# The last block of a channel-attention and SwiGLU kernel: twelve plain matmuls a step in place of twenty-one short ones

## The chip, the cores and the metric

The program runs on one core of one Trainium2 chip. The time is device microseconds (us) from the program's start to its end, lower is better. The core's engines have queues of their own, each worked off in order: TensorE (PE; its weight loads are shown apart as PEld), VectorE (DVE), ScalarE (ACT), GpSimd (POOL) and SyncE (SP), which only issues DMAs.

## The reference

```python
qn = q / (norm(q, axis=1) + 1e-6);  kn = k / (norm(k, axis=1) + 1e-6)     # (2, 6016, 256)
a = softmax(kn^T @ qn / tau)                                             # (2, 256, 256)
x = (v @ a).reshape(12032, 256)
xn = x / sqrt(mean(x*x) + 1e-6) * rms_g
out = (silu(xn @ w_gate) * (xn @ w_val)) @ w_out                         # d_ff = 1536
```

Everything is float32.

## The kernel before

A float32 operand is kept as the sum of two tiles of a rounded format (fp32r), a high and a low one, and a product of two operands is three matmuls: high by high, high by low, low by high. To make a pair of tiles out of a float32 tile, ScalarE copies it to the high tile and VectorE or GpSimd writes the difference to the low one.

The 12032 rows are 94 tiles of 128, worked off in 24 blocks: block 0 and block 23 have three tiles (384 columns of the transposed rows), the others four. In a block, step f = 0 to 11 makes a slice of 128 of the 1536 hidden columns, and five steps later (`LAG = 5`) that slice's part of the output is multiplied by `w_out` into PSUM.

There are two ways to compute a step. Blocks 0 and 1 are plain (`emit_hidden`): for gate and value, two slices of the 256 input columns times three matmuls, that is 12 matmuls over all columns of the block. Blocks 2 to 23 use a Strassen-Winograd scheme (`emit_step`): 7 products, each of three matmuls over half the columns (256, in block 23 it is 192), 21 in all. Its weight sums lie in the tiles `s` (`s_hl`), and for each pair p of steps the fourth sum has overwritten a quarter of the weights of step 2p+1 in place (`build_s`, the tile `w`). The output matmuls of some pairs use such a scheme too, and the plain output weights that it overwrote are restored in the last block by `restore_so`.

`emit_step` is a pipeline of three steps: at step f it runs products 7, 2 and 4 of step f-2, products 3 and 6 of step f-1 and products 5 and 1 of step f. Product 4 writes over a PSUM half (tile `pu`) that VectorE must have read before (line 771, the tiles `zg` and `zv`):

```python
product(7, u[:, 1])
...
nc.vector.tensor_tensor(out=z[:, 1:], in0=u, in1=t[:, :2], op=ALU.add)   # line 771
...
product(4, u[:, 1])
```

Line 772 adds product 2 (tile `pq`), line 790 multiplies gate by value for three of the four quarters, line 799 for the last. Line 696 turns the result for the output scheme (`run_turned`). `round_pair` then has it split into the pairs `gx`, `gy`, `gz`: ScalarE copies (line 704), GpSimd subtracts (line 710; on VectorE only for the last pair of block 23). `run_later` issues the parts of a pair that were put off. `post_copy`, `post_sums`, `post_out` and `post_store` read a finished block's output from PSUM (lines 931, 941, 950), turn it and store it; the next block writes to the same PSUM banks.

The order on every engine is the order in which the code issues (a manual schedule); the tables `steady`, `steady_mid` and `extra` say which side work follows which step. An instruction that waits holds up all that stand behind it on its engine.

Of the kernel before, what the change touches and what calls it, by code (L numbers as in the profile page):

```python
# [8 lines left out]
F32 = mybir.dt.float32  # L9
F32R = mybir.dt.float32r  # L10
# [5 lines left out]
P = 128  # L16
# [3 lines left out]
def kernel(  # L20
# [68 lines left out]
    def f32(ap):  # L89
        return ap.bitcast(F32)  # L90
# [469 lines left out]
    def emit_xT_round(j, i):  # L560
        h = blocks[j][2] * P // 2
# [103 lines left out]
    def round_pair(j, p, zg, h):  # L665

        x, y = new_g("x", 3, j, 2 * p), new_g("y", 2, j, 2 * p + 1)
        engine = nc.vector if (j, p) == (NB - 1, NP - 1) else nc.gpsimd
        w = [[w[:, 2 * p + i, e * P:(e + 1) * P] for w in wo] for i in range(2) for e in range(2)]
        if strassen(j, p):  # L670
            z = new_g("z", 2, j, 2 * p + 1)
# [12 lines left out]
        else:  # L684
            rounds.append((zg[:, 1:3], *(by_quarter(t, 2, h) for t in x), engine))
            later.append((zg[:, 0:4:3], *(by_quarter(t, 2, h) for t in y), engine))
            for i, g in enumerate((x, y)):
                if j == NB - 1:
                    G[j, 2 * p + i] = g
                    continue  # L690
# [118 lines left out]
    def new_state(j, f):  # L809
# [2 lines left out]
        t = pool["z"].tile([P, 3 * HN], F32, tag="t", name=f"t_{j}_{f}")  # L812
        return j, f, h, product, u, t[:, :3 * h].rearrange("p (i n) -> p i n", i=3)

    def emit_hidden(j, f, between=()):
        nt = blocks[j][2]
        n = nt * P
# [2 lines left out]
        for wj, nm in enumerate("gv"):  # L820
# [7 lines left out]
                    )  # L828
                    m += 1
            ps.append(t)  # L830
        if "z" not in pool:
# [7 lines left out]
        nc.vector.tensor_tensor(out=hh[:, :n], in0=th[:, :n], in1=ps[1][:, :n], op=ALU.mult)  # L839
        for go in between[1:]:  # L840
            go()
        tag = "xyz"[(j * NF + f) % 3]
        gh, gl = new_g(tag, 3 if tag == "x" else 2, j, f)
        rounds.append((hh[:, :n], gh[:, :n], gl[:, :n], nc.gpsimd if j else nc.vector))
        run_rounds()
        run_subs()
        G[j, f] = (gh, gl)
# [126 lines left out]
    with tc.manual_schedule():  # L974
# [128 lines left out]
        def at(j, f, go):  # L1103
            extra.setdefault((j, f), []).append(go)
# [51 lines left out]

        for i, f in enumerate((7, 7, 8)):
            at(NB - 1, f, lambda i=i: restore_so(i))

        def new_so():  # L1160
            so_hl.extend(
# [145 lines left out]
            go(0)  # L1307
            go(1)

        for i, (j, f) in enumerate(steps + [(None, None)] * 2):  # L1310
            outs = []
            if j is not None:
                owed.append((i + (2 if j < WINO else LAG), j, f))
            while owed and (owed[0][0] <= i or j is None and len(outs) < 2 and owed[0][1:] in G):
                outs.append(owed.pop(0)[1:])
            k = min(j, 5) if j is not None else None
            hooks = [
                [lambda go=go: go(j) for go in table[k].get(f, ())] if j is not None else []
                for table in (pres, mids, ends)
            ]  # L1320
# [52 lines left out]
```

## Time and profile before

| | |
|---|---|
| runs | 1266.56 us median of 3 (1266.0 to 1269.39) |
| the profiled execution | 1264.47 us, span 1262.7 us from its first to its last instruction |
| TensorE's granted clock | 0.999 of full speed |
| busy share of the span | PE 99%, PEld 94%, DVE 70%, ACT 69%, POOL 64% |
| block 23 | from about 1207 us to the end of the span |

A busy share is a mean over the span. Where one engine is busy nearly throughout, the others matter where it waits for them; a row of the timeline gives an instruction's start, its duration and, in square brackets, how long its engine stood idle before it and what ended that.

### The profile page before, as it was taken

How to read it: one execution, taken by the hardware profiler on the slowest of the kernel's cores; microseconds unless marked ns; L12 is line 12 of the kernel's file. 1: busy time of each engine (PE TensorE's matmuls, PEld its weight loads, DVE VectorE, ACT ScalarE, POOL GpSimd, SP SyncE). 2: the span in 40 equal slices, each digit the busy share in tenths (PEclk: the TensorE clock that was granted, in tenths of full speed). 3: DMA queues.
4: the chain of work that ended last, by engine and by line, in shares of the span. 5: the costliest groups of instructions: out<-in, count | busy, mean ns of one | idle time of the engine just before them, and what ended most of it. 6: DMA issues, size and time to landing. Idle time of an engine off the chain costs nothing.

```text
span 1262.7 us, 25136 instructions
## 1 busy us (share of the span) xinstructions
PE 1250.5 (99%) x9225; PEld 1191.4 (94%) x9225; DVE 885.8 (70%) x1573; ACT 868.4 (69%) x1771; POOL 803.5 (64%) x639
## 2 busy tenths in 40 slices
PE   8999999999999999999999999999999999999998
PEld 7799988999999999999999999999999999999998
DVE  5889698658767657667766766766676676676664
ACT  5667557667777787777767777777767767777654
POOL 0120355675777777777777777777877777777652
PEclk9999999999999999999999999999999999999999
DMA  8969111020220220211211211202202202101101
GB/s 305 321 215 288 31 35 49 19 36 18 52 34 18 50 35 18 47 33 24 44 25 35 39 29 36 38 21 45 35 18 51 35 18 51 30 18 30 18 1 30
DMA packets 223964, 71.77 MB, mean 57 GB/s; under 512 B 186592, under 2 KB 215392, under 8 KB 223840
## 3 DMA queue, kind: packets, MB, share of 16 engines
q1 hardware_dynamic: 223008, 68.92, 23.4%
q8 instruction: 72, 1.18, 0.4%
q10 hardware_dynamic: 832, 1.25, 0.3%
q14 instruction: 52, 0.43, 0.1%
HBM read 46.40 MB, written 12.32 MB: 47 GB/s over the span
## 4 chain that ended last, share of the span: by engine, by line
PE 91%; DVE 3%; DMA 2%; ACT 1%; SPq 1%; issue 1%; POOL 0%; POOLq 0%; ACTq 0%; DVEq 0%
PE pu L742 44%; PE po L916 26%; PE pq L742 7%; PE px L443 5%; PE s L180 3%; DMA raw<-in_k_dram 2%; PE po L866 2%; PE pg L825 1%; PE pv L825 1%; DVE wk L599 1%; SPq L532 1%; ACT sq L195 1%; DVE acc L204 0%; DVE zh L839 0%; PE pn L222 0%
## 5 line engine op out<-in xcount | busy, mean ns | idle before, releaser
L742 PE MATMUL pu<-xt,w 128*128 128x256 f32 (+1 forms) x2376 | 407.0, 280 | 0.4 <-DVE zv L771 0.3
L742 PE MATMUL pu<-xt,s 128*128 128x256 f32 (+1 forms) x2376 | 366.2, 280 | 0.9 <-ACT t L778 0.8
L742 PEld LDWEIGHTS pu<-xt,w 128*128 128x128 f32 x2376 | 343.8, 188 | 14.1 <-DVE zg L771 1.1
L742 PEld LDWEIGHTS pu<-xt,s 128*128 128x128 f32 x2376 | 326.8, 189 | 13.5 <-ACT t L778 1.0
L710 POOL TENSOR_TENSOR gy<-zg,gy 128x512 fp32r<-128x512 f32 (+1 forms) x131 | 181.6, 1386 | 150.3 <-ACT gy L704 82.9
L710 POOL TENSOR_TENSOR gx<-zg,gx 128x512 fp32r<-128x512 f32 (+2 forms) x131 | 200.3, 1529 | 83.0 <-ACT gx L704 82.8
L783 ACT ACTIVATE t<-pu 128x512 f32<-128x512 f32 (+1 forms) x264 | 156.9, 594 | 99.6 <-PE pu L742 83.1
L916 PE MATMUL po<-gx,w 128*128 128x256 f32 (+1 forms) x927 | 197.1, 330 | 0.0
L771 DVE TENSOR_TENSOR zv<-pu,t 128x512 f32<-128x512 f32 (+1 forms) x132 | 89.7, 679 | 102.7 <-ACT zg L805 76.8
L778 ACT ACTIVATE t<-pu 128x256 f32<-128x256 f32 (+1 forms) x264 | 100.1, 379 | 88.8 <-PE pu L742 87.1
L790 DVE TENSOR_TENSOR zg<-zg,zv 128x768 f32<-128x768 f32 (+1 forms) x132 | 150.0, 1136 | 13.7
L704 ACT ACTIVATE gx<-zg 128x512 fp32r<-128x512 f32 (+2 forms) x132 | 95.2, 721 | 71.7 <-DVE zg L799 37.0
L696 DVE TENSOR_TENSOR zg<-zg 128x256 f32<-128x256 f32 x228 | 97.0, 426 | 67.4 <-POOL gx L710 61.5
L916 PEld LDWEIGHTS po<-gx,w 128*128 128x128 f32 x927 | 136.4, 188 | 6.3 <-ACT os L952 0.2
L742 PE MATMUL pq<-xt,w 128*128 128x256 f32 (+1 forms) x792 | 135.7, 280 | 0.0
L771 DVE TENSOR_TENSOR zg<-pu,t 128x512 f32<-128x512 f32 (+1 forms) x132 | 89.0, 674 | 44.6 <-PE pu L742 29.1
L799 DVE TENSOR_TENSOR zg<-pu,zg 128x256 f32<-128x256 f32 (+1 forms) x132 | 55.6, 421 | 90.4 <-PE pu L742 88.6
L916 PE MATMUL po<-gy,w 128*128 128x512 f32 x414 | 118.1, 393 | 0.0
L710 POOL TENSOR_TENSOR gz<-zg,gz 128x512 fp32r<-128x512 f32 x57 | 114.1, 2001 | 0.0
L742 PEld LDWEIGHTS pq<-xt,w 128*128 128x128 f32 x792 | 111.9, 189 | 0.0
L787 ACT ACTIVATE zg<-zg 128x768 f32<-128x768 f32 (+1 forms) x132 | 109.5, 829 | 0.0
L572 POOL TENSOR_TENSOR xt<-xp,xt 128x512 fp32r<-128x512 f32 (+1 forms) x44 | 69.4, 1601 | 31.7 <-ACT xt L570 31.7
(146 smaller groups left out, 2051.7 us busy)
## 6 DMA issues: line engine op xcount, KB each, us to landing
v<-in_v_dram SPq DMA_DIRECT2D x84, 128.0 KB, 3.6
xnT<-xw SPq DMA_DIRECT2D x336, 32.0 KB, 1.9
out_dram<-ob SPq DMA_DIRECT2D x84, 128.0 KB, 3.2
raw<-in_q_dram SPq DMA_DIRECT2D x20, 512.0 KB, 4.9
raw<-in_k_dram SPq DMA_DIRECT2D x19, 512.0 KB, 5.9
wraw<-in_moe_w_gate_dram SPq DMA_DIRECT2D x12, 256.0 KB, 4.9
wraw<-in_moe_w_val_dram SPq DMA_DIRECT2D x12, 256.0 KB, 5.8
wraw<-in_moe_w_out_dram SPq DMA_DIRECT2D x12, 256.0 KB, 5.9
```

The costliest lines, as they stand in the source:

```text
L443: nc.tensor.matmul(out=px[:, i, :], lhsT=w[:, c, i * P:(i + 1) * P], rhs=x[:, c, :], start=(i == 0 and c == 0 and m == 0), stop=(c == KC - ...
L572: nc.gpsimd.tensor_tensor(out=o, in0=x, in1=f32(y), op=ALU.subtract)
L696: nc.vector.tensor_tensor(out=z[:, o], in0=z[:, i0], in1=z[:, i1], op=ALU.subtract)
L704: nc.scalar.activation(out=gh, in_=hh, func=AF.Copy)
L710: engine.tensor_tensor(out=gl, in0=hh, in1=f32(gh), op=ALU.subtract)
L742: nc.tensor.matmul(out=out, lhsT=wm[wi], rhs=xm[xi], start=(start and q == 0), stop=(q == 2), skip_group_check=True,)
L771: nc.vector.tensor_tensor(out=z[:, 1:], in0=u, in1=t[:, :2], op=ALU.add)
L778: nc.scalar.activation(out=mt[:, 0], in_=mu[:, 1], func=AF.Copy)
L783: nc.scalar.activation(out=nt[:, 1:], in_=nu, func=AF.Copy)
L787: nc.scalar.activation(out=zg[:, 1:], in_=zg[:, 1:], func=AF.Silu)
L790: nc.vector.tensor_tensor(out=zg[:, 1:], in0=zg[:, 1:], in1=z, op=ALU.mult)
L916: nc.tensor.matmul(out=acc[b][:, o:o + g.shape[-1]], lhsT=w, rhs=g, start=first, stop=True, skip_group_check=True,)
```

## The change

Block 23 is computed plainly. Its three tiles of input are split once as a whole (`emit_xT_round` calls `split`; the seven sums of the scheme fall away, `emit_xT_parts` returns). In its steps 0 and 1 the pipeline of block 22 is first run empty (`emit_step(None, None, ...)`), then `emit_hidden` issues the 12 matmuls of 384 columns. Steps 2 to 11 are `emit_hidden` and one output each. The two empty rounds of the pipeline behind the last step fall away. In block 23 VectorE, not GpSimd, subtracts for the low tile, and the split results lie in tiles that are no longer needed (`last_g`).

What the scheme had overwritten must be put back first: `restore_s(p)` computes the weights of step 2p+1 from three sums on VectorE, has ScalarE copy the high tile and VectorE write the low one. It stands behind steps 7 and 9 of block 22 (p = 0, 1) and behind steps 0, 2, 6 and 9 of block 23 (p = 2 to 5); step 2p+1 of block 23 needs it.

```diff
     def emit_xT_round(j, i):
+        if j == NB - 1:
+            if i == 0:
+                new_xT(j)
+                split(moved[j][:, :, :blocks[j][2] * P], xT[j], nc.gpsimd)
+            return
...
-        engine = nc.vector if (j, p) == (NB - 1, NP - 1) else nc.gpsimd
+        engine = nc.gpsimd
...
+    def restore_s(p):
+
+        t = pool["wk"].tile([P, 2, 2 * P], F32, tag="wk", name=f"wr_{p}")
+        wh, wl = (w[:, :, :2 * P] for w in w_hl)
+        sh, sl = (x[:, p, 0] for x in s_hl)
+        nc.vector.tensor_tensor(out=t[:, 0], in0=f32(wh[:, 2 * p]), in1=f32(wl[:, 2 * p]), op=ALU.add)
+        nc.vector.tensor_tensor(out=t[:, 1], in0=f32(sh), in1=f32(sl), op=ALU.add)
+        nc.vector.tensor_tensor(out=t[:, 0], in0=t[:, 0], in1=t[:, 1], op=ALU.subtract)
+        nc.scalar.activation(out=wh[:, 2 * p + 1], in_=t[:, 0], func=AF.Copy)
+        nc.vector.tensor_tensor(
+            out=wl[:, 2 * p + 1], in0=t[:, 0], in1=f32(wh[:, 2 * p + 1]), op=ALU.subtract
+        )
...
-        tag = "xyz"[(j * NF + f) % 3]
-        gh, gl = new_g(tag, 3 if tag == "x" else 2, j, f)
-        rounds.append((hh[:, :n], gh[:, :n], gl[:, :n], nc.gpsimd if j else nc.vector))
+        if j == NB - 1:
+            gh, gl = last_g(f)
+        else:
+            tag = "xyz"[(j * NF + f) % 3]
+            gh, gl = new_g(tag, 3 if tag == "x" else 2, j, f)
+        engine = nc.gpsimd if 0 < j < NB - 1 else nc.vector
+        rounds.append((hh[:, :n], gh[:, :n], gl[:, :n], engine))
...
+        for p, f in enumerate((7 - NF, 9 - NF, 0, 2, 6, 9)):
+            at(NB - 1 + f // NF, f % NF, lambda p=p: restore_s(p))
...
-        for i, (j, f) in enumerate(steps + [(None, None)] * 2):
+        for i, (j, f) in enumerate(steps):
...
-            if j is not None and j < WINO:
+            if j < WINO or j == NB - 1:
+                if j == NB - 1 and f < 2:
+                    emit_step(None, None, i % 2, outs)
+                    outs = []
+                elif j == NB - 1 and f == 2:
+                    run_later()
                 emit_hidden(j, f, weights.get((j, f), ()))
+                for go in hooks[1]:
+                    go()
                 for o in outs:
                     emit_all(o)
```

The change moves instructions on VectorE at two kinds of places. The first is VectorE's queue at step 7 of block 22, where step 5's results are finished and step 6's begin (line 799 is the last of step 5, line 771 the first of step 6). Before:

```order
L790 TENSOR_TENSOR zg_4_15307<-zg_4_15307,zv_5_15357 128x768 [waits DVE_49,Activation_49]
L799 TENSOR_TENSOR zg_4_15307<-pu_5_15251,zg_4_15307 128x256 [waits PE_49,Activation_49]
L771 TENSOR_TENSOR zg_6_15402<-pu_6_15298,t_6_15299 128x512 [waits PE_49,Activation_49,Pool_49]
L772 TENSOR_TENSOR zg_6_15402<-pq_6_15398,t_6_15299 128x256 [waits PE_49]
L696 TENSOR_TENSOR zg_4_15307<-zg_4_15307 128x256 [waits Pool_49]
L696 TENSOR_TENSOR zg_4_15307<-zg_4_15307 128x256 [waits DVE_49] x3
L771 TENSOR_TENSOR zv_7_15447<-pu_7_15346,t_7_15347 128x512 [waits PE_49,Activation_49]
```
After the change lines 771, 772, 790 and 799 have the numbers 775, 776, 794 and 803, and the four instructions of `restore_s(0)` are lines 842 to 846:

```order
L794 TENSOR_TENSOR zg_4_15301<-zg_4_15301,zv_5_15347 128x768 [waits DVE_49,Activation_49]
L803 TENSOR_TENSOR zg_4_15301<-pu_5_15245,zg_4_15301 128x256 [waits PE_49,Activation_49]
L842 TENSOR_TENSOR wr_15383<-w_97,w_98 128x256
L843 TENSOR_TENSOR wr_15383<-s_1413,s_1414 128x256
L844 TENSOR_TENSOR wr_15383<-wr_15383 128x256 [waits DVE_49]
L846 TENSOR_TENSOR w_98<-wr_15383,w_97 128x256 [waits Activation_49]
L775 TENSOR_TENSOR zg_6_15398<-pu_6_15292,t_6_15293 128x512 [waits PE_49,Pool_49]
L776 TENSOR_TENSOR zg_6_15398<-pq_6_15394,t_6_15293 128x256 [waits PE_49]
L700 TENSOR_TENSOR zg_4_15301<-zg_4_15301 128x256 [waits Pool_49]
```
Four instructions now stand between step 5's last and step 6's first, and the fourth of them waits for ScalarE. The same holds behind step 9 with `restore_s(1)`.

The second place is VectorE's queue where block 23 begins. `pu_11` is the PSUM tile of block 22's step 11, `pu_0` that of block 23's step 0. Before:

```order
L696 TENSOR_TENSOR zg_8_15496<-zg_8_15496 128x256 [waits DVE_49] x3
L771 TENSOR_TENSOR zv_11_15647<-pu_11_15535,t_11_15536 128x512 [waits PE_49,Activation_49]
L772 TENSOR_TENSOR zv_11_15647<-pq_11_15643,t_11_15536 128x256 [waits PE_49]
L790 TENSOR_TENSOR zg_10_15596<-zg_10_15596,zv_11_15647 128x768 [waits DVE_49,Activation_49]
L799 TENSOR_TENSOR zg_10_15596<-pu_11_15535,zg_10_15596 128x256 [waits PE_49,Activation_49]
L771 TENSOR_TENSOR zg_0_15693<-pu_0_15587,t_0_15588 128x384 [waits PE_49,Activation_49,Pool_49]
```
After, `zh_0` is step 0's plain result (line 876), `glast_0` its low tile (line 714), and `wr` belongs to `restore_s(2)`:

```order
L700 TENSOR_TENSOR zg_8_15498<-zg_8_15498 128x256 [waits DVE_49] x3
L876 TENSOR_TENSOR zh_0_15641<-zh_0_15641,pv_0_15634 128x384 [waits PE_49,Activation_49]
L714 TENSOR_TENSOR glast_0_15645<-zh_0_15641,glast_0_15644 128x384 [waits Activation_49]
L842 TENSOR_TENSOR wr_15648<-w_97,w_98 128x256
L843 TENSOR_TENSOR wr_15648<-s_1413,s_1414 128x256
L844 TENSOR_TENSOR wr_15648<-wr_15648 128x256 [waits DVE_49]
L846 TENSOR_TENSOR w_98<-wr_15648,w_97 128x256 [waits Activation_49]
L775 TENSOR_TENSOR zv_11_15665<-pu_11_15537,t_11_15538 128x512 [waits PE_49]
L776 TENSOR_TENSOR zv_11_15665<-pq_11_15661,t_11_15538 128x256 [waits PE_49]
L794 TENSOR_TENSOR zg_10_15596<-zg_10_15596,zv_11_15665 128x768 [waits DVE_49]
```
The reading of `pu_11`, which stood directly behind `run_turned` (line 696, now 700), now stands behind block 23's step 0, its split and a restoration.

## Rows read from the trace of the kernel before

**Rows 1.** The page's busy times (part 1): busy us, share of the span, instructions.
```profile
PE 1250.5 (99%) x9225; PEld 1191.4 (94%) x9225; DVE 885.8 (70%) x1573; ACT 868.4 (69%) x1771; POOL 803.5 (64%) x639
```

**Rows 2.** Waits from 1207 us on, TensorE's weight loads: total us, times, longest.
```profile
PEld po L866 <- POOL gy L710: 0.6, 1, 0.6
PEld pu L742 <- DVE zg L771: 0.3, 1, 0.3
PEld po L866 <- DVE gx L710: 0.3, 1, 0.3
PEld po L866 <- ACT gx L704: 0.3, 1, 0.3
```

**Rows 3.** Timeline, TensorE's weight loads in block 23: start, us, engine, line, tiles.
```profile
1228.85 0.75 PEld L742 LDWEIGHTS pu<-xt,s 128*128 128x128 f32 x6
...
1229.86 0.78 PEld L866 LDWEIGHTS po<-w,gy 128*128 128x128 f32 x6
...
1230.57 0.42 PEld L742 LDWEIGHTS pu<-xt,w 128*128 128x128 f32 x3
...
1232.27 0.75 PEld L742 LDWEIGHTS pu<-xt,s 128*128 128x128 f32 x6
```

**Rows 4.** Timeline, TensorE in block 0, matmuls of 384 columns.
```profile
119.13 1.20 PE L825 MATMUL pv<-xt,w 128*128 128x384 f32 x6
120.17 1.23 PE L866 MATMUL po<-w,gx 128*128 128x256 f32 x9
```

**Rows 5.** Timeline of all engines, block 22, step 7.
```profile
1190.72 0.42 DVE L799 TENSOR_TENSOR zg<-pu,zg 128x256 f32<-128x256 f32 x1
...
1191.27 0.85 ACT L704 ACTIVATE gx<-zg 128x768 fp32r<-128x768 f32 x1 [1.01 <-DVE zg L799]
...
1192.19 1.85 POOL L710 TENSOR_TENSOR gx<-zg,gx 128x768 fp32r<-128x768 f32 x1 [0.35 <-ACT gx L704]
...
1193.73 0.54 PEld L742 LDWEIGHTS pu<-xt,w 128*128 128x128 f32 x3
```

**Rows 6.** Timeline of all engines, block 22, step 9.
```profile
1197.06 2.01 POOL L710 TENSOR_TENSOR gz<-zg,gz 128x512 fp32r<-128x512 f32 x1
...
1198.33 0.42 DVE L799 TENSOR_TENSOR zg<-pu,zg 128x256 f32<-128x256 f32 x1 [0.41 <-PE pu L742]
...
1199.80 1.84 POOL L710 TENSOR_TENSOR gx<-zg,gx 128x768 fp32r<-128x768 f32 x1 [0.73 <-ACT gx L704]
...
1201.26 0.42 PEld L742 LDWEIGHTS pu<-xt,w 128*128 128x128 f32 x3
```

**Rows 7.** Lines 605 and 602: count, duration in ns as min/median/max, starts.
```profile
L605 DVE TENSOR_TENSOR w<-wk,w x6: 421/1513/1517, 163.6 to 226.9; 128x256 fp32r<-128x256 f32 x6
L602 ACT ACTIVATE w<-wk x6: 403/419/422, 161.6 to 224.9; 128x256 fp32r<-128x256 f32 x6
```

**Rows 8.** Timeline, the restoring of out weights that the kernel already has.
```profile
1235.53 1.32 POOL L710 TENSOR_TENSOR gx<-zg,gx 128x384 fp32r<-128x384 f32 x1 [2.40 <-ACT gx L704]
...
1236.02 1.25 DVE L646 TENSOR_TENSOR wback<-wback,wback 128x384 f32<-128x384 f32 x1
...
1237.78 0.41 PEld L742 LDWEIGHTS pu<-xt,w 128*128 128x128 f32 x3 [0.31 <-DVE zg L771]
```

**Rows 9.** Groups by form, block 0's chain at 384 columns: busy us, mean ns.
```profile
L836 ACT ACTIVATE th<-pg 128x384 f32<-128x384 f32 x12 | 5.8, 479 | 0.0
...
L839 DVE TENSOR_TENSOR hh<-th,pv 128x384 f32<-128x384 f32 x12 | 6.5, 545 | 0.0
...
L704 ACT ACTIVATE gx<-hh 128x384 fp32r<-128x384 f32 x4 | 2.1, 525 | 3.4 <-DVE hh L839 3.4
...
L710 DVE TENSOR_TENSOR gx<-hh,gx 128x384 fp32r<-128x384 f32 x4 | 2.2, 547 | 0.0
```

**Rows 10.** Timeline, block 22's sums on VectorE.
```profile
1224.52 1.29 DVE L950 TENSOR_TENSOR os<-po,os 128x512 f32<-128x512 f32 x2 [0.70 <-PE po L916]
```

**Rows 11.** Windows, the end: us; busy us of PE, PEld, DVE, ACT, POOL; PEclk; DMA.
```profile
1258.00:1262.70 4.70, 0.33 (x3) 0.13 (x2) 0.42 (x1) 0.27 (x1) 0.00 (x0) 0.77 0.32 84
```

More of the change, by code (lines that the diff above doesn't have):

```diff
@@ L560, in emit_xT_round @@
     def emit_xT_round(j, i):
+        if j == NB - 1:
+            if i == 0:
+                new_xT(j)
+                split(moved[j][:, :, :blocks[j][2] * P], xT[j], nc.gpsimd)
+            return
         h = blocks[j][2] * P // 2
@@ L687, in round_pair @@
             for i, g in enumerate((x, y)):
-                if j == NB - 1:
-                    G[j, 2 * p + i] = g
-                    continue
                 G[j, 2 * p + i] = [(e, 0, w[2 * i + e], [t[:, :2 * h] for t in g]) for e in range(2)]
@@ L813, in new_state, with last_g @@
         return j, f, h, product, u, t[:, :3 * h].rearrange("p (i n) -> p i n", i=3)
+    spare = {}
+    def last_g(f):
+        n = BN
+        if 4 <= f < 8:
+            if f == 4:
+                spare["xt"] = [
+                    xt_p.tile([P, XS * HN], F32R, tag=f"xt{i}", name=f"glast{i}") for i in range(2)
+                ]
+            n = XS * HN // 4
+            return [x[:, (f - 4) * n:(f - 3) * n] for x in spare["xt"]]
+        if f % 4 < 2:
+            p, tag = ((vt_p, "vt"), (sm_p, "a"))[f % 4]
+            return [p.tile([P, n], F32R, tag=f"{tag}{i}", name=f"glast{i}_{f}") for i in range(2)]
+        x = xn_p.tile([P, 2, n], F32R, tag=("xn", "moved")[f % 2], name=f"glast_{f}")
+        return [x[:, i] for i in range(2)]
+    def restore_s(p):
[9 more added lines that the diff above has]
+        )
     def emit_hidden(j, f, between=()):
@@ L830, in emit_hidden @@
             ps.append(t)
-        if "z" not in pool:
+        if (j, f) == (NB - 1, 0):
+            th = hh = v_p.tile([P, BN], F32, tag="vw", name=f"zh_{j}_{f}")
+        elif "z" not in pool:
             th, hh = (pool["h"].tile([P, BN], F32, tag=y, name=f"{y}_{j}_{f}") for y in ("th", "hh"))
@@ L841, in emit_hidden @@
             go()
-        tag = "xyz"[(j * NF + f) % 3]
-        gh, gl = new_g(tag, 3 if tag == "x" else 2, j, f)
-        rounds.append((hh[:, :n], gh[:, :n], gl[:, :n], nc.gpsimd if j else nc.vector))
+        if j == NB - 1:
+            gh, gl = last_g(f)
[4 more added lines that the diff above has]
+        rounds.append((hh[:, :n], gh[:, :n], gl[:, :n], engine))
         run_rounds()
@@ L1308, in emit_all @@
             go(1)
-        for i, (j, f) in enumerate(steps + [(None, None)] * 2):
+        for i, (j, f) in enumerate(steps):
             outs = []
-            if j is not None:
-                owed.append((i + (2 if j < WINO else LAG), j, f))
-            while owed and (owed[0][0] <= i or j is None and len(outs) < 2 and owed[0][1:] in G):
+            owed.append((i + (2 if j < WINO else LAG), j, f))
+            while owed and owed[0][0] <= i:
                 outs.append(owed.pop(0)[1:])
-            k = min(j, 5) if j is not None else None
+            k = min(j, 5)
             hooks = [
-                [lambda go=go: go(j) for go in table[k].get(f, ())] if j is not None else []
-                for table in (pres, mids, ends)
-            ]
-            if j is not None and j < WINO:
+                [lambda go=go: go(j) for go in table[k].get(f, ())] for table in (pres, mids, ends)
+            ]
+            if j < WINO or j == NB - 1:
[4 more added lines that the diff above has]
+                    run_later()
                 emit_hidden(j, f, weights.get((j, f), ()))
+                for go in hooks[1]:
+                    go()
                 for o in outs:
@@ L1332 @@
                 go()
-            for go in extra.get((j, f), []) if j is not None else []:
+            for go in extra.get((j, f), []):
                 go()
-        run_later()
         owed = [emit_out(*o[1:]) for o in owed]
```

## Prediction

> **What bounds the kernel now.** I read the page's busy times first: TensorE is busy 99% of the span [rows 1], so what counts is the length of its queue and every wait in it; the other engines cost something only where it waits for them. Next came the waits of the stretch that changes, from 1207 us to the end: its weight loads waited 0.6 us for GpSimd and three times 0.3 us, 1.5 us in all [rows 2]. Then the timeline, for the price of a step. In block 23 the same group of six weight loads starts at 1228.85 and again at 1232.27, so a step takes 3.42 us [rows 3]. Its six output matmuls take the time to the next group, 1230.57 - 1229.86 = 0.71, so 0.118 each; nine take 1.06. The 21 products of 192 columns have the other 2.36 us, 0.112 each.
>
> The plain form is in the trace too, in block 0 with the same 384 columns: six start at 119.13, the next group at 120.17, so 0.173 each and 2.08 for twelve [rows 4].
>
> **What is gained.** 2.36 - 2.08 = 0.28 a step, 3.3 us over 12 steps. The last pairs, which had to come through the pipeline's two empty rounds, were what TensorE waited for in rows 2; a plain step's result is ready while four other outputs are still to be multiplied (4 x 0.71 = 2.8 us). I take off the 1.5 us too. Gain: 4.8 us.
>
> **What is added.** Work for ScalarE and VectorE, which have room on average. But both are strict queues, and a plain step with its restoration goes back and forth between them. The prices: SiLU 0.48, product 0.55, copy 0.53, subtraction 0.55 [rows 9]; in a restoration an operation of 128x256 on VectorE 0.42 at best, ScalarE's copy 0.41 [rows 7]. A hand-over takes some 0.1: line 799 ends at 1191.14, ScalarE starts at 1191.27, and GpSimd 0.07 behind ScalarE's end [rows 5]. From TensorE's last weight load to the reader I reckon 0.4 (an estimate: in rows 4 the matmuls run 1.20 us where their group has 1.04, plus the hand-over).
>
> *Restoration 0, behind step 7 of block 22.* VectorE is free at 1191.14 [rows 5]. Three operations: 1192.4. ScalarE's copy: 1192.9. The last subtraction reads two tiles in SBUF, as GpSimd does, and GpSimd's `gx` is due at 1192.19. Such a pair gets in each other's way: VectorE's subtraction of line 605 took 0.42 us or 1.51 [rows 7], and line 646 took 1.25 beside a GpSimd operation, where one of that size alone takes 0.55 [rows 8, 9]. If `gx` starts when the third operation is done, it runs to 1192.4 + 1.85 = 1194.25, the subtraction to 1194.7, line 771 (0.6 until TensorE can go on) to 1195.3. TensorE wants product 4 at 1193.73: it waits 1.6 us. Bounds: 0.3 if nothing gets in the way, 2.4 if `gx` comes in before the third operation.
>
> The Trainium skill ("SBUF — State Buffer", section "SBUF: two separate sides") says that VectorE with two inputs in SBUF and GpSimd share a port pair as an exclusive lock, held for a whole instruction. The 1.51 and 1.25 above agree. By this rule the wait would be the 1.6 and the sum below stands; if the two went on side by side at half speed, the subtraction would take 0.84 from 1192.97 on, the wait would be 0.7, and the sum 0.9 less.
>
> *Restoration 1, behind step 9.* VectorE is free at 1198.75, GpSimd's `gz` runs to 1199.07, and `gx` is due at 1199.80 [rows 6]. Two operations fit between them (1199.9), then either the third or `gx` comes. With `gx` first it ends at 1201.75, the third at 1202.2, the copy at 1202.7, the subtraction at 1203.2, line 771 at 1203.8. TensorE wants product 4 at 1201.26: 2.5 us. With the third first it is 2.0, without any meeting 0.5, and if restoration 0's delay has pushed `gz` back against line 799, 3.2. I take 2.4.
>
> *The emptied pipeline, steps 0 and 1 of block 23.* In step 1 product 4 of block 22's step 11 waits for line 771, and that now stands behind step 0 and restoration 2 (the second place under the change). From the last weight load of step 0, VectorE and ScalarE need 0.4 + 0.55 (product) + 0.1 + 0.53 (copy) + 0.05 + 0.55 (subtraction) + 1.25 (three operations) + 0.1 + 0.41 (copy) + 0.05 + 0.42 + 0.6 (line 771) = 5.0 us. TensorE has products 7 and 2 (six, 0.71) and five output matmuls (0.59), then needs it: 1.3 us of cover. It waits 3.7. GpSimd is through with `gx` by then, so nothing meets here. Bounds: 1.5 if the restoration cost nothing there, 4.3 with a meeting.
>
> *Block 22's output, step 5.* Block 23's first output needs PSUM banks that line 950 has read. Now the sums ahead of it (four operations, 1.7) come behind step 4's subtraction. After the last output matmul of block 22 (call it T): 0.75 to the subtraction's end, 1.7, and 0.65 for the first half of line 950 [rows 10]: T + 3.1, 0.1 more for the hand-over. TensorE covers one plain step, 2.1. It waits 1.1; bounds 0 and 1.9.
>
> *Restoration 5, behind step 9.* A step costs TensorE 2.08 + 1.06 = 3.14 us. From step 5 to step 9 the two engines have a round of 1.8 us for each step, and besides these the rest of line 950, the turning of block 22's output (1.3), restorations 4 and 5 (2.3 each with their hand-overs) and `restore_so` (2.7). Laid out in order from T + 3.75, step 9's subtraction ends at T + 20.7 and the high tile of restoration 5 at T + 22.4; TensorE, with the wait above, comes to step 11 at T + 19.9. It waits 2.5; bounds 0 and 2.9. The earlier restorations 2 to 4 have two or more steps to spare. The outputs at the end have enough cover.
>
> **The sum.** -4.8 + 1.6 + 2.4 + 3.7 + 1.1 + 2.5 = +6.5 us on the profiled execution's 1264.47 (span 1262.7 and 1.8 around it): 1271.0. The median of the runs lies 2.1 above that execution, 1266.56; I give the forecast on it: 1273.1 us, 0.5% slower. A difference of 0.3% (3.8 us) is about what a measurement tells from none. All low ends together give -2.5, all high ends +9.9.
>
> **The rivals.**
> 1. *VectorE and GpSimd don't meet in block 22.* Then restorations 0 and 1 cost 0.3 and 0.5, the sum is +3.3, 1269.9 us. For it: line 605 had the 0.42 as well [rows 7]. Against: its median is 1.51, and `gx` is due 0.2 us before the third operation ends.
> 2. *TensorE's clock falls during a wait.* In the last 4.7 us it had three matmuls, and the granted clock was 0.77 on the mean [rows 11]; between levels 1 (2.4 GHz) and 0.5 (1.2 GHz) that is nearly half of the time at the lower. A wait of 3.7 us is about as long. What follows then takes twice as long until the clock rises; for one step (2.08 + 0.4) 2.5 us more, an estimate: 1275.6. Against it: before, there is hardly a wait to show it in mid-program. The Trainium skill ("TensorE: Matmul & The Clock Gate", section "What's actually happening") has the gate let half of the pulses through after an idle stretch. By this rule the rival holds wherever a wait is long enough; no run here shows for how long.
> 3. *Not slower: line 771 comes in time.* Place: VectorE's queue in step 1 of block 23. If line 771 is done when TensorE gets to product 4, 1.3 us behind step 0's end, 3.7 us fall away: +2.8, 1269.4, within 0.3%. It decides at 1.3 us. For it: only queue order is against it, and VectorE is busy 70%. Against: the order shows step 0's product ahead of line 771, and this alone ends no earlier than 0.95 us after step 0, line 771 at 1.6.
> 4. *TensorE's queue alone decides*, the others always being ahead: -4.8, 1261.8, faster. Against it: the kernel's own restoration already held TensorE up 0.31 us [rows 8], with three operations where there are now four and a hand-over back.
>
> **How the numbers follow.** Forecast 42%, clock 20%, no meeting 16%, line 771 in time 12%, TensorE alone 10%. Slower by over 0.3%: the first two and a third of the third, 68%. Within: the rest of the third and the fourth, 22%. Faster: 10%. The range reaches from 1267, below rivals 1 and 3, to 1278.5, above the clock's case with the high ends; it leaves out rival 4 and little else.
>
> **What would show it.** After the change: about 0.173 us for a plain matmul; waits of TensorE for line 775 (771 now) of 1.6 and 2.4 us in block 22 and of 3.7 us in block 23, for line 991 (950) of 1.1 us, for line 845 (the restored high tile) of 2.5 us ahead of step 11; operations of 1.2 us and more on line 846 in block 22. I would be wrong if TensorE goes through block 23 without a gap, or if the restorations in block 22 take 0.42 us an operation.

## The result, and the profile after

The changed kernel takes 1273.71 us (median, 1272.36 to 1276.11) where the kernel before took 1266.48 in the same sitting: a ratio of 1.0052, 95% interval 1.004 to 1.0064. It is slower, by about what was forecast (1273.1). In the profile after, line 771 of before is line 775, 742 is 746, 825 is 860, 866 is 907, 916 is 957, 950 is 991; the restoration is lines 842 to 846.

The waits of TensorE's weight loads from 1180 us on are the five that the prediction lists, and no others; those of before [rows 2] are gone. The timeline of the weight loads (in brackets the idle time ahead and what ended it) has them in their order: restorations 0 and 1, the emptied pipeline, block 22's output, and restoration 5 with its high and its low tile.

```profile
1198.38 0.41 PEld L746 LDWEIGHTS pu<-xt,w 128*128 128x128 f32 x3 [1.28 <-DVE zg L775]
...
1208.45 0.42 PEld L746 LDWEIGHTS pu<-xt,w 128*128 128x128 f32 x3 [2.59 <-DVE zg L775]
...
1223.07 0.42 PEld L746 LDWEIGHTS pu<-xt,w 128*128 128x128 f32 x3 [3.42 <-DVE zv L775]
...
1223.97 1.82 PEld L860 LDWEIGHTS pg<-xt,w 128*128 128x128 f32 x6
1225.79 1.70 PEld L860 LDWEIGHTS pv<-xt,w 128*128 128x128 f32 x6
1227.47 1.06 PEld L860 LDWEIGHTS pg<-xt,w 128*128 128x128 f32 x6
...
1241.11 1.13 PEld L907 LDWEIGHTS po<-w,glast 128*128 128x128 f32 x9 [1.11 <-DVE os L991]
1242.17 1.00 PEld L860 LDWEIGHTS pg<-xt,w 128*128 128x128 f32 x6
1243.16 1.06 PEld L860 LDWEIGHTS pv<-xt,w 128*128 128x128 f32 x6
1244.20 1.19 PEld L907 LDWEIGHTS po<-w,glast 128*128 128x128 f32 x9
...
1259.30 0.30 PEld L860 LDWEIGHTS pg<-xt,w 128*128 128x128 f32 x2 [1.31 <-ACT w L845]
1259.76 0.64 PEld L860 LDWEIGHTS pg<-xt,w 128*128 128x128 f32 x4 [0.16 <-DVE w L846]
```

A plain step's twelve matmuls take 2.03 us (1242.17 to 1244.20, where the next group starts), 0.17 each as in block 0 [rows 4]. The pair at 1223.97 takes 3.50 instead. The windows of that stretch show why (PEclk is the third column from the right):

```profile
1223.00:1224.00 1.00, 0.93 (x7) 0.93 (x8) 0.97 (x3) 0.00 (x0) 1.00 (x2) 0.88 0.00 0
1224.00:1225.00 1.00, 1.00 (x5) 1.00 (x5) 1.00 (x2) 0.17 (x1) 1.00 (x1) 0.50 0.00 0
...
1227.00:1228.00 1.00, 1.00 (x7) 1.00 (x7) 0.09 (x1) 0.00 (x0) 0.09 (x1) 0.91 0.00 0
```

The granted clock is 1 up to 1223, so through nearly all of the wait of 3.42 us, falls to 0.5 (1.2 GHz) some 0.7 us after TensorE has gone on, and is back in the window from 1227. The pair lost 3.50 - 2.03 = 1.47 us by it. That is rival 2, smaller than it was priced.

Where the spans differ: the same group of block 22, ahead of every restoration, starts here in before, after, and in the rearranged kernel e10 below. From block 0's first 384-column matmul to this row TensorE takes the same time in all three, 1112.46 to 1112.48 us.

```profile
1183.20 0.53 PEld L742 LDWEIGHTS pu<-xt,s 128*128 128x128 f32 x3
```
```profile
1186.61 0.53 PEld L746 LDWEIGHTS pu<-xt,s 128*128 128x128 f32 x3
```
```profile
1183.74 0.53 PEld L746 LDWEIGHTS pu<-xt,s 128*128 128x128 f32 x3
```

To the spans' ends (1262.7, 1271.8, 1257.6) that leaves 79.50, 85.19 and 73.86 us. So 5.69 us of the 9.1 by which the two spans differ arose behind this row; the other 3.4 was there at block 0's first 384-column matmul already, in code that is the same. There the profiled execution of before (70.72, the changed kernel's 74.15) is earlier than those of all the other kernels here (71.28 to 76.06). The medians differ by 7.2.

### The profile page after: what moved, and what is told of

Read it like the earlier page. It is cut to its first block, busy times and chain, and to the rows that moved or that the text cites. A ratio compares the mean times of both kernels' runs of the same rounds, so it can differ in the third digit from the quotient of the medians.

```text
span 1271.8 us, 24858 instructions
## 1 busy us (share of the span) xinstructions
PE 1252.3 (98%) x9117; PEld 1192.3 (94%) x9117; DVE 893.0 (70%) x1583; ACT 861.1 (68%) x1750; POOL 789.2 (62%) x623
## 3 DMA queue, kind: packets, MB, share of 16 engines
q8 instruction: 71, 1.16, 0.4%
## 4 chain that ended last, share of the span: by engine, by line
PE 91%; DVE 3%; DMA 2%; ACT 1%; issue 1%; SPq 1%; POOL 0%; ACTq 0%; DVEq 0%; POOLq 0%
PE pu L746 42%; PE po L957 26%; PE pq L746 7%; PE s L180 5%; PE px L443 5%; PE pg L860 2%; PE pv L860 2%; DMA raw<-in_k_dram 2%; PE po L907 2%; DVE wk L606 1%; SPq L532 1%; DVE zh L876 0%; DVE wr L844 0%; ACT glast L708 0%; DVE wr L842 0%
## 5 line engine op out<-in xcount | busy, mean ns | idle before, releaser
L746 PE MATMUL pu<-xt,w 128*128 128x256 f32 x2268 | 389.5, 280 | 6.8 <-DVE zv L775 3.5
L746 PE MATMUL pu<-xt,s 128*128 128x256 f32 x2268 | 350.5, 281 | 0.9 <-ACT t L782 0.8
L714 POOL TENSOR_TENSOR gy<-zg,gy 128x512 fp32r<-128x512 f32 x126 | 176.2, 1398 | 151.7 <-ACT gy L708 82.9
L714 POOL TENSOR_TENSOR gx<-zg,gx 128x768 fp32r<-128x768 f32 (+1 forms) x126 | 195.8, 1554 | 74.2 <-ACT gx L708 73.9
L787 ACT ACTIVATE t<-pu 128x512 f32<-128x512 f32 x252 | 151.2, 600 | 97.7 <-PE pu L746 78.1
L794 DVE TENSOR_TENSOR zg<-zg,zv 128x768 f32<-128x768 f32 x126 | 145.2, 1152 | 13.0
L782 ACT ACTIVATE t<-pu 128x256 f32<-128x256 f32 x252 | 96.2, 382 | 78.4 <-PE pu L746 76.9
L708 ACT ACTIVATE gx<-zg 128x768 fp32r<-128x768 f32 (+1 forms) x126 | 92.1, 731 | 67.3 <-DVE zg L803 35.3
L746 PE MATMUL pq<-xt,w 128*128 128x256 f32 x756 | 129.8, 280 | 0.0
L791 ACT ACTIVATE zg<-zg 128x768 f32<-128x768 f32 x126 | 105.5, 837 | 0.4 <-DVE zg L776 0.4
```

What stands on the lines that cost most here:

```text
L708: nc.scalar.activation(out=gh, in_=hh, func=AF.Copy)
L714: engine.tensor_tensor(out=gl, in0=hh, in1=f32(gh), op=ALU.subtract)
L746: nc.tensor.matmul(out=out, lhsT=wm[wi], rhs=xm[xi], start=(start and q == 0), stop=(q == 2), skip_group_check=True,)
L782: nc.scalar.activation(out=mt[:, 0], in_=mu[:, 1], func=AF.Copy)
L787: nc.scalar.activation(out=nt[:, 1:], in_=nu, func=AF.Copy)
L791: nc.scalar.activation(out=zg[:, 1:], in_=zg[:, 1:], func=AF.Silu)
```

## The experiments

Each ratio is to the kernel before, measured beside it; the changed kernel's is 1.0052. The diffs are against the changed kernel.

**e1, no restoration.**

```diff
-        for p, f in enumerate((7 - NF, 9 - NF, 0, 2, 6, 9)):
-            at(NB - 1 + f // NF, f % NF, lambda p=p: restore_s(p))
```

> The six restorations of weight tiles are left out, so block 23's first products are computed with weight tiles that are not restored; all else is as in the changed kernel. Theory (the waits are the restorations' time on VectorE and ScalarE): the waits of 1.28 and 2.59 us for line 775 in block 22 shrink to 0.3 each or less, the 1.47 us ahead of step 11 is gone, the 3.42 us wait in block 23 shrinks by the restoration's 2.2 us to about 1.2, the half clock behind it (some 1.5 us) goes too, and the 1.1 us for line 991 stays. Together 8 to 9 us less than 1273.7: 1264.5 to 1266, at or a little below the kernel before. Rival A (the emptied pipeline alone is what holds TensorE up): the 3.42 us stay, only 1.28 and 2.59 and 1.47 go, 1268.4. Rival B (the first matmul's later start, 74.2 us for 70.7, belongs to the change and not to one execution): it starts at 74 here as well and 3 us of the difference stay.

1264.05 us, ratio 0.9982 (0.9974 to 0.9991). The waits from 1175 us on:

```profile
PEld pu L746 <- DVE zv L775: 1.4, 1, 1.4
PEld po L907 <- DVE os L991: 1.1, 1, 1.1
```

As the theory said, and 0.5 us below its range. Three waits and the half clock are the restorations', and 2.0 of the 3.42 us. Without them the plain block is a small gain. Rival B falls too: the first matmul of block 0 does start at 73.4 here, and yet the time is below that of the kernel before.

**e2, the pipeline emptied first.**

```diff
-                if j == NB - 1 and f < 2:
-                    emit_step(None, None, i % 2, outs)
+                if j == NB - 1 and f == 0:
+                    emit_step(None, None, 0, outs)
+                    emit_step(None, None, 1, [owed.pop(0)[1:]])
                     outs = []
```

> Only the place of the two emptying rounds is changed: both ahead of block 23's step 0, so that line 775 of block 22's step 11 stands ahead of step 0's product, its copy and its subtraction and of restoration 2. Theory (queue order makes the 3.42 us wait, and the wait makes the half clock): the wait falls to about 0.7 us, the two groups of six 384-column matmuls behind it take 1.0 us each for the 1.8 and 1.7 now, the other four waits stay: 2.7 to 4.2 us less, 1269.5 to 1271. Rival A (the wait is the pipeline's own latency, whatever stands between): it stays over 2.5 us, 1272.8 or more. Rival B (the half clock comes from something other than the wait): the wait falls and the groups stay at 1.7 to 1.8, 1271.

1270.35 us, ratio 1.0028 (1.0017 to 1.004). The wait fell to 1.16 (0.7 forecast), so queue order made most of it; the wait for line 991 grew from 1.11 to 1.46. The 1.16 that is left looks like queue order too: the matmuls of product 7 end at 1216.59, but line 775 starts only at 1217.74, behind four subtractions of `run_turned` (line 700) that had waited for GpSimd. No run tested this by itself.

```profile
1216.03 1.80 DVE L700 TENSOR_TENSOR zg<-zg 128x256 f32<-128x256 f32 x4 [1.47 <-POOL gx L714]
1217.74 0.68 DVE L775 TENSOR_TENSOR zv<-pu,t 128x512 f32<-128x512 f32 x1
```

With the shorter wait the clock stayed up there. But in this execution it fell behind the wait of 2.60 us in block 22, which was in the changed kernel's profile without such a fall:

```profile
1206.71 0.71 PEld L746 LDWEIGHTS pu<-xt,w 128*128 128x128 f32 x3 [2.60 <-DVE zg L775]
```
```profile
1207.00:1208.00 1.00, 1.00 (x6) 1.00 (x6) 0.93 (x3) 0.89 (x2) 0.00 (x0) 0.50 0.00 0
```

**e3, restorations 0 and 1 in one, one step earlier.**

```diff
+        at(NB - 2, 6, restore_two)   # tiles [P, 4, 2 * P]: both pairs in each operation
-        for p, f in enumerate((7 - NF, 9 - NF, 0, 2, 6, 9)):
+        for p, f in ((2, 0), (3, 2), (4, 6), (5, 9)):
```

> Restorations 0 and 1 are made together, by operations of twice the width, behind step 6 of block 22, where VectorE stands idle 1.58 us and GpSimd 2.8 us. Theory (each restoration of block 22 costs by one chain of hand-overs that meets GpSimd's subtractions): the waits of 1.28 and 2.59 us become one of at most 0.6, 3.3 us less, 1270.4. Rival A (VectorE simply has too much to do in block 22, place and number of chains don't matter): the 3.9 us are waited for at the steps behind, no change, 1273.7. Rival B (operations of twice the width meet GpSimd just as well): one wait of 1.5 to 3, 1272 to 1273.

1270.57 us, ratio 1.0027 (1.0017 to 1.0038). Beside an idle GpSimd each operation of twice the size takes 0.69, and the one wait left in block 22 is 0.58:

```profile
1190.37 0.69 DVE L845 TENSOR_TENSOR wr<-wr 128x512 f32<-128x512 f32 x1
```

The waits of block 23 are as before, so VectorE had the room (rival A falls). Place and number of chains were changed together; this run doesn't tell which of the two counts.

**e4, restorations 2 to 5 on GpSimd.**

```diff
+        engine = nc.gpsimd if p > 1 else nc.vector
-        nc.vector.tensor_tensor(...)
+        engine.tensor_tensor(...)
```

> Restorations 2 to 5 run on GpSimd in place of VectorE, which GpSimd has nothing else to do beside, in block 23; ScalarE's copy, and restorations 0 and 1, stay as they are. Theory (it is the queue of VectorE that is late): the 3.42 us wait falls to about 1.7, with it the half clock behind it if 2.6 us without a matmul leave the clock at 1 as in block 22, and the 1.47 us ahead of step 11 go: 3.2 to 4.7 us less, 1269 to 1270.5. Rival A (GpSimd's operations get in the way of VectorE's as in block 22, 1.5 us for 0.42): the wait for line 775 stays over 3 us and some more come at later steps, 1273 or more. Rival B (ScalarE's copy is late, not VectorE): the waits stay, 1273.7.

1274.85 us (1270.62 to 1276.62), ratio 1.0057 (1.0043 to 1.0072): the theory was wrong.

```profile
PEld pu L746 <- DVE zv L775: 2.2, 1, 2.2
PEld pg L861 <- ACT w L846: 2.0, 1, 2.0
PEld po L908 <- DVE os L992: 2.0, 1, 2.0
```

Below, first VectorE beside a restoration on GpSimd, then the start of restoration 5 on GpSimd:

```profile
1214.64 3.17 DVE L700 TENSOR_TENSOR zg<-zg 128x256 f32<-128x256 f32 x4 [1.05 <-POOL gx L714]
```
```profile
1253.66 0.74 POOL L843 TENSOR_TENSOR wr<-w,w 128x256 f32<-128x256 f32 x1 [6.15 <-DVE w L657]
```

The wait in block 23 got shorter (2.23 for 3.42), the later ones longer (1.96 for 1.11, and ahead of step 11 2.03 and 0.51 for 1.31 and 0.16): GpSimd needs 0.74 us for what VectorE does in 0.42, it holds VectorE's own work up (four subtractions of line 700 took 3.17 where they take 1.80), and restoration 5 could not start before line 657 had given back the one work buffer. In the profiled execution (1271.23 us) the clock never fell in these blocks. Its mean granted clock is 0.999; the four executions of 1274.29 us and more have 0.995 to 0.997, so the trace shows one of the two short ones of six, and what the clock did in the others is not shown.

**e6, e9, e11: what the meeting with GpSimd costs.** In the changed kernel the two restorations of block 22 stand thus beside GpSimd (VectorE, then GpSimd):

```profile
1196.18 1.55 DVE L846 TENSOR_TENSOR w<-wr,w 128x256 fp32r<-128x256 f32 x1 [0.49 <-ACT w L845]
...
1203.40 1.18 DVE L842 TENSOR_TENSOR wr<-w,w 128x256 f32<-128x256 f32 x1
...
1204.95 1.94 DVE L844 TENSOR_TENSOR wr<-wr 128x256 f32<-128x256 f32 x1
```
```profile
1195.60 1.85 POOL L714 TENSOR_TENSOR gx<-zg,gx 128x768 fp32r<-128x768 f32 x1 [2.84 <-ACT gx L708]
...
1202.29 2.01 POOL L714 TENSOR_TENSOR gz<-zg,gz 128x512 fp32r<-128x512 f32 x1
1204.51 2.09 POOL L714 TENSOR_TENSOR gx<-zg,gx 128x768 fp32r<-128x768 f32 x1 [0.22 <-ACT gx L708]
```

Each long operation ends 0.3 us behind a GpSimd operation's end (1197.73 and 1197.45, for one). e6 gave VectorE one input only:

```diff
     def restore_s(p):
+        if p < 2:
...
+            nc.vector.tensor_copy(t[:, 0], f32(wh[:, 2 * p]))
+            nc.vector.tensor_copy(t[:, 1], f32(sh))
+            nc.vector.tensor_copy(t[:, 0], t[:, 1])
...
```

> In restorations 0 and 1 alone each VectorE operation reads one tile in place of two (four copies of the same size, at the same places, with the same hand-overs to ScalarE); the rest is the changed kernel. These two restorations are so left out in effect, and the first columns of block 23 are computed with other weights. Theory (VectorE's two-input operations are held up by GpSimd's, one at a time): line 846 takes 0.5 us or less for 1.55, the operations of restoration 1 0.5 or less for 1.18 and 1.94, GpSimd's subtractions beside them stay, and the waits of 1.28 and 2.59 us become at most 0.4 and 0.7: 1270 to 1271. Rival (what is waited for is the chain's hand-overs and queue places, not the meeting): the waits stay over 1 and 2 us, 1273 or more.

1272.48 us, ratio 1.0046 (1.0033 to 1.0059), waits 1.14 and 2.08. A copy takes 0.28 alone (line 844), but meets GpSimd just as a subtraction does:

```profile
1195.90 1.73 DVE L847 CAST w<-w 128x256 fp32r<-128x256 f32 x1 [0.56 <-ACT w L846]
...
1203.30 1.05 DVE L843 COPY wr<-w 128x256 f32<-128x256 f32 x1
...
1204.59 1.82 DVE L845 COPY wr<-wr 128x256 f32<-128x256 f32 x1
```

So two inputs are not what it takes, and this run told neither theory nor rival. The Trainium skill ("SBUF — State Buffer", section "SBUF: two separate sides") counts a float32 copy within SBUF among the operations that take the shared port pair, and lets two inputs count only against a GpSimd operation that reads SBUF. e9 and e11 therefore leave VectorE as it was and let GpSimd write without reading:

```diff
+        engine = None if j == NB - 2 and p in (3, 4) else nc.gpsimd      # e9; (2, 3) in e11
...
+            if engine is None:
+                nc.gpsimd.memset(f32(gl), 0.0)
+                continue
```

> The restorations are those of the changed kernel. What is changed is GpSimd's share beside them: its four subtractions nearest to restorations 0 and 1 in block 22 (two tiles in SBUF read each) become fills with zero of the same target tiles, which read nothing in SBUF; the low parts of those results are so left out. The run with one-input copies had left the question open: its copies still took 1.73, 1.05 and 1.82 us beside GpSimd. Theory (it is the meeting with GpSimd's reads that stretches line 842 to 846, and the stretched operations are what TensorE waits for): all eight operations take 0.42 to 0.45 us and the waits are those of the case forecast without a meeting, 0.3 and 0.5 us at most, for 1.28 and 2.59: 1270.5. Rival (the chain with its hand-overs is too long even unstretched): operations of 0.42 us, and waits of 1 and 1.5 us that stay: 1272 or more.

> As the run before with the zero fills, but for the four subtractions of GpSimd that really lie beside the two restorations (in the last run three of the four lay behind them, and that of restoration 0 was not among them): the third-to-last pairs' x, y and z parts and the next pair's x part. Their low parts are left out. Theory (the meeting alone): lines 842 to 846 take 0.42 to 0.45 us in both restorations, that of 1.55 in restoration 0 and of 1.18 in restoration 1 too; the first wait falls from 1.28 by 1.13 to 0.2 at most, the second from 1.07 by 0.76 to 0.3 at most, the later waits stay: 1269.5 to 1270.5. Rival (hand-overs and queue places set a floor): the waits stay at 0.8 and 0.8 or more though the operations take 0.42.

e9: 1270.85 us, ratio 1.003 (1.0018 to 1.0041). Of its fills only one lay beside a restoration. Restoration 0 was unchanged (1.55, wait 1.28); in restoration 1 line 848, the changed kernel's 844, took 0.42 for 1.94, and the wait was 1.07 for 2.59: 1.52 less, by exactly the 1.52 that the operation was shorter.

```profile
1203.20 0.42 DVE L848 TENSOR_TENSOR wr<-wr 128x256 f32<-128x256 f32 x1
```
```profile
1205.20 0.42 PEld L750 LDWEIGHTS pu<-xt,w 128*128 128x128 f32 x3 [1.07 <-DVE zg L779]
```

e11: 1269.35 us, ratio 1.0016 (1.0007 to 1.0025); all eight operations 0.42 to 0.43, the waits 0.15 and none:

```profile
1196.70 0.42 DVE L847 TENSOR_TENSOR wr<-s,s 128x256 f32<-128x256 f32 x1
...
1198.06 0.42 DVE L850 TENSOR_TENSOR w<-wr,w 128x256 fp32r<-128x256 f32 x1 [0.48 <-ACT w L849]
...
1203.98 0.42 DVE L846 TENSOR_TENSOR wr<-w,w 128x256 f32<-128x256 f32 x1
```
```profile
1196.73 0.74 POOL L716 MEMSET gx<- 128x768 f32 x1 [2.09 <-PE po L961]
...
1204.13 0.74 POOL L716 MEMSET gx<- 128x768 f32 x1 [2.54 <-PE po L961]
```

The fills ran at the same time as some of VectorE's operations (lines 847 and 846 above) and stretched none. Line 850 of restoration 0, the one that had taken 1.55, had no operation of GpSimd beside it any more. So the meeting with GpSimd's subtractions is shown as the cause of both waits: 3.72 us of waiting went, 3.41 of it by the shorter operations; line 794 ahead of restoration 1 (798 here) got shorter too, 0.96 for 1.73, and 0.15 us is left. That it is GpSimd's reading, the overlapped operations show. The Trainium skill's rule, as given above, agrees with all three runs.

**e7, the sums one step earlier; e8, restoration 5 early.**

```diff
-            3: (hi, v1),
-            4: (sums_, c0, c1),
+            3: (hi, last_sums, v1),          # e7: block 22's sums
+            4: (other_sums, c0, c1),
```
```diff
-        for p, f in enumerate((7 - NF, 9 - NF, 0, 2, 6, 9)):
+        for p, f in enumerate((7 - NF, 9 - NF, 0, 2, 6)):
...
+        at(NB - 1, 1, lambda: restore_s(5, None, None, "t"))      # e8: a buffer of its own
```

> Only the four sums of block 22's output stand one step earlier, behind step 3 of block 23; the rest is the changed kernel. Theory (the sums stand between step 4's subtraction and line 991, 1.67 us of VectorE): the 1.11 us wait for line 991 goes, nothing else grows, 1272.6. Rival (VectorE is behind in steps 2 to 4 anyway): the wait stays, or the same time is waited at a plain step's banks, 1273.7.

> Only restoration 5 is moved, from behind step 9 to behind step 1 of block 23, into a buffer of its own; the rest is the changed kernel. Theory (it comes too late by its place, behind a VectorE queue that is a step and a half late): the 1.47 us ahead of step 11 go, the wait for line 991 stays at 1.1, 1272.2. Rival (VectorE's arrears, which keep step 9 and 10 late in any case): another wait of about 1.5 us takes its place, for the banks of steps 9 to 11 or for line 991, 1273.7.

e7: 1272.62 us, ratio 1.0046 (1.0034 to 1.0057), the wait for line 991 is 0.68 for 1.11. e8: 1273.96 us, ratio 1.0051 (1.0039 to 1.0063): the wait ahead of step 11 is gone, that for line 991 (1000 there) is 1.77 for 1.11.

```profile
1243.05 1.12 PEld L907 LDWEIGHTS po<-w,glast 128*128 128x128 f32 x9 [0.68 <-DVE os L991]
```
```profile
1242.93 1.13 PEld L916 LDWEIGHTS po<-w,glast 128*128 128x128 f32 x9 [1.77 <-DVE os L1000]
```

Both lie between theory and rival. In e7 the sums (line 982) only change places with step 4's product and subtraction, and all of these still stand ahead of line 991 in VectorE's queue; in e8 restoration 5 is added ahead of it. From step 2's product to step 5's (1231.44 to 1241.57 in the changed kernel) VectorE never waits for TensorE, only for ScalarE's copies, 0.49 and 0.59 us at a time, so work put in there, or right ahead of it, comes back as waiting in part. Times this close to the changed kernel's don't tell; the rows do.

**e5 and e10, rearranged.** `restore_s` takes a part here (0: the three operations, 1: copy and last subtraction), an engine, and a buffer of the emptied pipeline.

```diff
+        at(NB - 2, 6, lambda: restore_s(0))
+        for f, p, part, engine in (                                       # e10
+            (0, 1, 0, nc.vector), (1, 1, 1, nc.vector), (1, 2, 0, nc.vector), (2, 2, 1, nc.vector),
+            (2, 3, 0, nc.gpsimd), (3, 3, 1, nc.gpsimd), (5, 4, 0, nc.gpsimd), (6, 4, 1, nc.gpsimd),
+            (7, 5, 0, nc.gpsimd), (8, 5, 1, nc.gpsimd),
+        ):
...
+                if j == NB - 1 and f == 0:
+                    banks[0] = 0                                          # e10
+                    emit_step(None, None, 0, outs)
+                    emit_step(None, None, 1, [owed.pop(0)[1:]], (), [lambda: emit_hidden(NB - 1, 0)])
...
+                elif j == NB - 1 and f == 4:                              # e10
+                    for o in outs:
+                        emit_all(o)
+                    outs = []
+                    post_out(NB - 2, 0)
+                    post_out(NB - 2, 1)
```

> The change with every restoration kept, but placed where the traces show room: restoration 0 behind step 6 of block 22; the pipeline emptied ahead of block 23, with step 0's twelve plain matmuls between step 11's product 2 and product 4, so that they cover the 1.2 us that the emptied pipeline still cost by itself; restorations 1 to 3 in two pieces (three operations behind one step, copy and last subtraction behind the next) on VectorE behind steps 0 to 3, restorations 4 and 5 so on GpSimd from steps 3 and 6 on; the four sums of block 22 one step earlier, behind step 3. Theory (the plain form gains its 3.3 us and the 1.5 of the old last pairs, all that was lost are waits that order makes): no wait over 0.6 us in blocks 22 and 23, no half clock there, 1261 to 1263, that is 0.3 to 0.45% below the kernel before. Rival A (VectorE has too little room for the restorations wherever they stand): waits of 2 us or more somewhere in block 23, 1265 or more. Rival B (the clock falls whatever the waits): half clock without a wait ahead of it, 1263 to 1266.

e5: 1265.93 us, ratio 0.9991 (0.9983 to 1.0). The five waits were gone, and two others there. A wait of 2.1 us and 1265.93 us are the numbers of rival A (too little room on VectorE), not the theory's; e10 tests whether it is room or order:

```profile
PEld pg L869 <- DVE zv L776: 2.1, 1, 2.1
PEld po L916 <- DVE os L1000: 1.5, 1, 1.5
```

> The rearranged kernel again, with what its trace showed mended: step 0's two products take banks that are free (the 2.10 us wait was for the bank of product 2's quarter, which line 776 has yet to read); in step 4 block 22's last output matmuls and both halves of its sum stand ahead of the plain products, so that line 1000 (991 in the changed kernel) doesn't wait behind step 4's product and subtraction; restoration 3 goes from VectorE to GpSimd, and 4 and 5 start two and one steps later. Theory (both waits were order, and TensorE's queue is the bound when they are gone): no wait over 0.7 us in block 23, 3 us less than the rearranged kernel's 1265.9: 1262 to 1263.5, 0.3 to 0.4% below the kernel before. Rival A (VectorE is a step behind and is the bound there): the wait for line 1000's successor stays over 1.5 us or comes back at a plain step's banks, 1264 or more. Rival B (restorations 3 to 5 on GpSimd come too late): a wait for a restored tile at step 7, 9 or 11 of 1 us or more, 1264.

e10: 1260.93 us (1259.76 to 1261.83), ratio 0.9953 (0.994 to 0.9967), faster than both kernels and 1.1 us below the low end of its forecast. From 1165 us on its weight loads wait for nothing, and the clock stays at 1 from 1200 to 1256 us; two stretches of it, and one plain step:

```profile
1210.00:1220.00 10.00, 10.00 (x69) 10.00 (x69) 8.57 (x18) 4.95 (x10) 4.93 (x4) 1.00 0.00 0
1220.00:1230.00 10.00, 10.00 (x58) 9.46 (x58) 8.02 (x15) 3.35 (x9) 6.28 (x8) 1.00 0.01 2
```
```profile
1229.43 1.00 PEld L869 LDWEIGHTS pg<-xt,w 128*128 128x128 f32 x6
...
1231.46 1.19 PEld L916 LDWEIGHTS po<-w,glast 128*128 128x128 f32 x9
1232.58 1.00 PEld L869 LDWEIGHTS pg<-xt,w 128*128 128x128 f32 x6
```

VectorE is 86% and 80% busy in these two stretches, and TensorE doesn't wait: a busy VectorE was not the bound. Some of that is meetings with GpSimd, which go on here: two operations of the restorations take 1.33 and 1.52 us for 0.42 (lines 849 and 850, at 1215.35 and 1219.67). Here, where TensorE doesn't wait for them, they cost it nothing.

## Why the prediction was right, step by step

Behind the common row of block 22, e10 is the plain block without a wait: 73.86 us. The changed kernel's waits are 1.28 + 2.59 + 3.42 + 1.11 + 1.47 = 9.87, the clock 1.47: 73.86 + 11.34 = 85.20, where its trace has 85.19. Nothing is left over. The other traces agree: from the same row to the span's end, less the waits that follow it, are 73.8 to 73.9 us in e1, e4 and e5, where the clock doesn't fall on the way, 75.2 to 75.6 in e2, e3, e6, e8, e9 and e11, where it falls once, and 78.0 in e7, where it falls twice.

- **The gain**, forecast 4.8, is 79.50 - 73.86 = 5.64. The step was right: 3.15 us (1229.43 to 1232.58) for 3.42 [rows 3], 3.2 over twelve, and before's waits behind the row, 1.46 [rows 2]. What the term left out is the tail: the span ends 3.7 us behind the last matmul (1253.94 to 1257.6) where before took 4.4. Some 0.2 has no place.
- **Restorations 0 and 1**: 1.6 and 2.4 forecast, 1.28 and 2.59 measured, in the way described: the last operation of restoration 0 met GpSimd, and in restoration 1 `gx` came in ahead of the third. The first operation there was held by `gz` for 0.76 us, where the layout had 0.3. Rival 1 (no meeting, 0.3 and 0.5) is what e11 shows, as another kernel.
- **The emptied pipeline**: 3.7 forecast, 3.42 measured; 2.0 of it restoration 2's (e1); 1.2 stays with restoration and step 0 out of the way (e2), with line 700 still ahead of line 775, and step 0's matmuls cover it (e10). The 0.4 from the last load to its reader, of which the prediction's working gives 0.16 and 0.1, is 0.4 in the trace (1218.25 to 1218.67). Rival 3 fell.
- **Block 22's output**: 1.1 and 1.11. In e8 and e4 it came near the high bound of 1.9 (1.77 and 1.96).
- **Restoration 5**: the term that was mis-sized, 2.5 for 1.47. From T (1237.8, the end of block 22's last output loads) TensorE came to step 11 at T + 20.2, near the T + 19.9 of the prediction; the high tile was ready at T + 21.4, a full 1.0 sooner than "T + 22.4". Some half of it is the layout: the prices given, from step 6's product at T + 6.7 on, put the end of step 9's subtraction at T + 20.2, not at T + 20.7. The rest is prices that were too high: a step's round takes VectorE 1.62 us (1249.67 to 1251.29 in the rows below) for the 1.8 reckoned, a restoration 2.08 (1247.59 to 1249.67) for 2.3, since an operation starts a little before its forerunner's recorded end (lines 842 and 843 start 0.34 us apart and take 0.43 and 0.42). `restore_so`, with 0.97 us in which VectorE waits for ScalarE, took more than its 2.7, some 3.1.

```profile
1236.53 1.29 PEld L957 LDWEIGHTS po<-gy,w 128*128 128x128 f32 x6
```
```profile
1247.59 0.43 DVE L842 TENSOR_TENSOR wr<-w,w 128x256 f32<-128x256 f32 x1
...
1249.67 0.56 DVE L876 TENSOR_TENSOR zh<-zh,pv 128x384 f32<-128x384 f32 x1
...
1251.29 0.55 DVE L651 TENSOR_TENSOR wback<-so,so 128x384 f32<-128x384 f32 x1
```

- **The clock**: rival 2 had 20% and 2.5 us. It happened, at 1.47. Sum forecast +6.5; from the row on +5.69 measured, since a larger gain and a smaller restoration 5 paid for it. So what happened is rival 2's case, and the number came out as that of the main case, which had no fall of the clock: in that it was luck. The waits themselves were foreseen, each in its place.

What stays open: the medians differ by 7.2, the two traces by 5.7 behind the row. The rest may be the start, which differs by some us between executions, or a second fall of the clock behind the wait of 2.59 in other runs (the granted clock of the changed kernel's runs is 0.993 to 0.997); neither was shown. For the start the traces have a hint: the clock falls ahead of block 0 in some executions and not in others. The three traces without such a fall (before, e9, e10) reach block 0's first matmul at 70.7 to 72.4 us, the five with one fall at 72.3 to 74.2, and the five with half speed for twice as long, the changed kernel's among them, at 73.4 to 76.1. Whether the fall makes the late start or comes of it, no run tested.

## What to carry to other kernels

Price a preparatory step by the queue that it stands in and by what its neighbour engine reads at that moment, not by the mean load of its engine: waits and half clock took 11 us of TensorE's time in the changed kernel, 9 of them for the restorations, and none in e10, with the same operations in another order and three of the six restorations on another engine. When a pipeline is emptied ahead of work of another form, put the first of that work inside the emptying, into banks that the pipeline no longer needs, and give every preparation a buffer of its own so that it can start when its data, not a neighbour's buffer, is free. e10 did all of this at once; what each part is worth was not measured. A wait that is taken away can come back in part at another place, so read which is next (e5, e8).

## What the runs showed of the hardware that was not expected

- The clock falls behind some waits and not behind others of the same length. Behind the wait of 3.41 to 3.42 us in block 23 it fell in all seven profiled executions that have it (the changed kernel, e3, e6, e7, e8, e9, e11). Behind that of 2.59 to 2.60 us it fell in two of five (e2 and e7, not the changed kernel, e4, e8), and behind none of 2.03 to 2.23 us (e4 twice, e5, e6). It falls from 1.0 us before TensorE goes on (e7) to 1.5 us after (e7 too, behind its wait of 2.60). In e7 the half speed behind the longer wait lasted twice as long as in the changed kernel, to 1230.2.
- A VectorE copy of float32 from SBUF to SBUF, with one input, is held up by GpSimd's subtraction like an operation with two (1.05 to 1.82 us for 0.28, e6), while GpSimd's fill with zero held up none of the two-input operations beside it (0.42 us, e11).
